# A shorter first softmax, and all taps of the first 32 columns summed on TensorE

## The chip, the cores and the metric

One core of one Trainium2 chip. The metric is the time of one execution on the device in microseconds (us), best read as a ratio to the kernel before, run in the same rounds on the same chip. Before: 417.61 us, median of 3 runs (417.58 to 418.06).

## The reference

Two stages, on 8 x 4160 tokens of 192 numbers. A dynamic convolution weighs, for each token and each of 8 heads, the token and its 6 predecessors with a softmax of 7 logits; then a maxout layer takes the larger of two products with 192 x 1024 weights and multiplies it by a third matrix.

```
w = exp(weight_gen - max);  w = w / sum(w)              # 8 heads x 7 taps
conv[b,s,h,:] = sum_k w[b,s,h,k] * x_pad[b,s+k,h,:]     # 24 channels a head
g = maximum(conv @ w1, conv @ w2)                       # 192 -> 1024
out = g @ w_out                                         # 1024 -> 192
```

## The kernel before

Each of the 128 partitions holds 260 consecutive tokens ("columns"), worked off in batches of 16. The work of a batch runs through the engines like this; the names are those of the profile:

```
exp_sum(b)     ScalarE  e_t = exp(wg_t)
red(b)         VectorE  sum_t = sums of 7
ln(b)          ScalarE  sum_t = ln(sum_t)
shift(b)       VectorE  wg_t -= sum_t          # from batch 3 on in 3 parts, between the additions
weights(b, o)  ScalarE  en_t = exp(wg_t)       # columns o..: the softmax weights, each twice
mul(b, o)      VectorE  m_t = x * en_t         # 7 taps x 8 columns x 192, 5.75 us
adds(b, o)     VectorE  the 7 taps added up into y_t
transpose(u)   DMA      yt = y_t transposed    # the "features" of TensorE
hidden(g, ..)  TensorE  hd = yt * (w2 - w1); ScalarE: rd_t = relu(hd)
               TensorE  op_ps = w1 w_out, yt + w_out, rd_t; ScalarE: o_t = op_ps, then the store
```

So two chains pass through ScalarE in turn: VectorE's (sum, logarithm, subtraction, exps, product) and TensorE's (features, relus, results). In the traces ScalarE runs its instructions in the order in which they are written: one that waits holds up what stands behind it (by 4.62 us in one case below).

The first 32 columns (batches 0 and 1) go in pieces of four, and TensorE itself transposes them and adds up taps, by multiplying m_t with the identity:

```python
LEFT = (0, 1, 2, K - 1)

def sum_transpose(u, taps=range(K)):
    ...
    for k in range(6):
        for t in taps:
            for r in range(2):
                ...
                nc.tensor.matmul(yps[:, ...], lhsT=m_t[half(r), at:at + P],
                                 rhs=ident[half(r), half(r)], ...)
    nc.scalar.copy(out=_sub(yt, ...), in_=_sub(yps, ...))

# later batches, hung on tile t of the hidden layer:
if s == 0 and b + 1 < NB:
    c = b + 1
    mul(c, 0)
    adds(c, 0, beside=lambda i, of: shift(c + 1, i, of) if c + 1 < NB else None)
if s == 8 and b + 2 < NB:
    mul(b + 1, 8)
    adds(b + 1, 8, beside=lambda i, of: red(b + 3, i, 2) if b + 3 < NB and i < 2 else None)
```

Five of the eight pieces go with LEFT: VectorE adds three taps onto three others (`adds(.., True)`), and TensorE sums four. The other three leave all seven to TensorE.

The softmax here doesn't subtract the row's maximum and nothing guards it: scores larger than these inputs give would overflow.

Of the kernel before, what the change touches and what calls it, by code (L numbers as in the profile page):

```python
# [9 lines left out]
FP32 = mybir.dt.float32  # L10
# [3 lines left out]
ALU = mybir.AluOpType  # L14
# [9 lines left out]
def kernel(  # L24
# [100 lines left out]
    def exp_sum(b):  # L125
        e_ts[b] = pe_.tile([P, BATCHES[b][1] * WGC], FP32, name="e_t", tag="e")
        nc.scalar.activation(out=e_ts[b], in_=wg_ts[b], func=AF.Exp)  # L127

    def part(b, i, of):

        n = BATCHES[b][1]
        h0, h1 = n * i // of * H, n * (i + 1) // of * H
        return slice(h0, h1), h0 * K, [[K, h1 - h0], [1, K]]

    def red(b, i=0, of=1):
        if i == 0:
            s_ts[b] = psm.tile([P, BATCHES[b][1] * H], FP32, name="sum_t", tag="sum")
        hs, at, ap = part(b, i, of)
        nc.vector.reduce_sum(out=s_ts[b][:, hs], in_=_sub(e_ts[b], at, ap), axis=AX.X)  # L139

    def ln(b):
        nc.scalar.activation(out=s_ts[b], in_=s_ts[b], func=AF.Ln)  # L142

    def shift(b, i=0, of=1):
        hs, at, ap = part(b, i, of)
        w_t = _sub(wg_ts[b], at, ap)
        nc.vector.tensor_tensor(out=w_t, in0=w_t, in1=_sub(s_ts[b], hs.start, [[1, hs.stop - hs.start], [0, K]]),  # L147
                                op=ALU.subtract)

    def weights(b, o):  # L150

        w = dict(pieces(b))[o]
        if b not in en_ts:
            en_ts[b] = pen.tile([P, 16 * WGC * 2], BF16, name="en_t", tag="en")
        J = 2 if w == 4 and b < 2 else 1
        N = w * H // J
        for j in range(J):
            nc.scalar.activation(  # L158
                out=_sub(en_ts[b], (o * WGC + j * N * K) * 2, [[2 * N, K], [2, N], [1, 2]]),
                in_=_sub(wg_ts[b], (o * H + j * N) * K, [[1, K], [K, N], [0, 2]]), func=AF.Exp,  # L160
            )


    def mul(b, o):

        n = dict(pieces(b))[o]
        if n == 4 and b < 2:
            m_out = _sub(m_t, K * o * D, [[64, 2], [P, K * 6], [1, 64]])
            x_in = _sub(xb_ts[b], o * D, [[2 * D, 2], [D, K], [1, 2 * D]])
        else:  # L170
            m_out = m_t[:, K * o * D:K * (o + n) * D]
            x_in = _sub(xb_ts[b], o * D, [[D, K], [1, n * D]])
        nc.vector.tensor_tensor(  # L173
            out=m_out, in0=x_in,
            in1=_sub(en_ts[b], o * WGC * 2, [[2, K * n * H], [0, G // 2], [1, 2]]),
            op=ALU.mult,
        )

    def adds(b, o, first=False, beside=lambda i, of: None):


        w = dict(pieces(b))[o]
        n = w * D

        def taps(at, step, cnt):
            return _sub(m_t, K * o * D + at * n, [[step * n, cnt], [1, w * D]])

        beside(0, 3)
        nc.vector.tensor_tensor(out=taps(0, 1, 3), in0=taps(0, 1, 3), in1=taps(3, 1, 3), op=ALU.add)  # L189
        if first:  # L190
            return
        beside(1, 3)
        if b not in y_ts:
            y_ts[b] = py.tile([P, 16 * D], BF16, name="y_t", tag="y")
        nc.vector.tensor_tensor(out=taps(0, 2, 2), in0=taps(0, 2, 2), in1=taps(1, 5, 2), op=ALU.add)  # L195
        beside(2, 3)

        nc.vector.tensor_tensor(  # L198
            out=_sub(y_ts[b], o * D, [[64, 2], [P, 3 * w // 2], [1, 64]]),
            in0=taps(0, 1, 1), in1=taps(2, 1, 1), op=ALU.add,  # L200
        )
# [24 lines left out]
    LEFT = (0, 1, 2, K - 1)  # L226

    def sum_transpose(u, taps=range(K)):

        b, o, n = UNITS[u]  # L230
        assert n == 4
        yps = ps["r" if "r" in ps else "o"].tile([P, 1024], FP32, name="yps", tag="op")
        for k in range(6):
            for t in taps:
                for r in range(2):
                    at = (K * o + t * n) * D + k * P
                    nc.tensor.matmul(  # L237
                        yps[:, r * 512 + k * 64:r * 512 + (k + 1) * 64],
                        lhsT=m_t[half(r), at:at + P], rhs=ident[half(r), half(r)],
                        start=(k == 0 and t == taps[0]), stop=(t == taps[-1]),  # L240
                        skip_group_check=True,
                    )
        yt = pyt.tile([P, 8 // 2 * 3 * P], BF16, name="yt", tag="yt")
        nc.scalar.copy(out=_sub(yt, 0, [[64, 2], [P, 6], [1, 64]]),  # L244
                       in_=_sub(yps, 0, [[512, 2], [64, 6], [1, 64]]))
        yt_ts[u] = yt

# [143 lines left out]
    OUTS, c = [[], [], []], 0  # L391
    for g in range(3, len(GROUPS)):
        most = 4 if g == 3 else 2 if GROUPS[g][1] == 2 or len(OUTS[-1]) == 4 else 4
        n = min(most, ready[g] - c)
        OUTS.append(list(range(c, c + n)))
        c += n
# [78 lines left out]
    with tc.tile_pool(name="pstage", bufs=1) as pstage:  # L475
# [5 lines left out]
        load_wg(0, nc.sync)  # L481
# [14 lines left out]
        load_first(0)  # L496
        HF = F // 2

        def load_w(h):
            for kind, r0, nr in (("E", 0, P), ("T", P, 64)):  # L500
                for wi, wsrc in enumerate((moe_w1, moe_w2)):
# [17 lines left out]
        exp_sum(0)  # L519
        red(0)  # L520
        ln(0)
        shift(0)
        xb_ts[0] = pxb.tile([P, (16 + PAD) * D], BF16, name="xb_t", tag="xb")
        nc.scalar.activation(out=xb_ts[0][:, 0:PAD * D], in_=xs[:, 0:PAD * D], func=AF.Copy,
                             scale=msk[:, 0:1])
        for o in (0, 4, 8, 12):
            weights(0, o)
        nc.vector.tensor_copy(out=xb_ts[0][:, PAD * D:(PAD + 4) * D],
                              in_=xs[:, PAD * D:(PAD + 4) * D])
        mul(0, 0)  # L530
        nc.scalar.copy(out=xb_ts[0][:, (PAD + 4) * D:(PAD + 8) * D], in_=xs[:, (PAD + 4) * D:])
# [3 lines left out]
        def w_diff(h, copy):  # L535

            c0, c1, c2 = (slice(s * F + h * HF, s * F + (h + 1) * HF) for s in range(3))
            nc.vector.tensor_tensor(out=wd[:, c0], in0=ws["E", 1][:, c0], in1=ws["E", 0][:, c0],
                                    op=ALU.subtract)
            copy(out=wd[64:P, c2], in_=wd[0:64, c0])  # L540
            copy(out=wd[0:64, c1], in_=wd[64:P, c0])
            nc.vector.tensor_tensor(out=wd[0:64, c2], in0=ws["T", 1][:, c0], in1=ws["T", 0][:, c0],
                                    op=ALU.subtract)
            copy(out=wd[64:P, c1], in_=wd[0:64, c2])


        nc.gpsimd.tensor_copy(out=gate[0:64, :], in_=ws["T", 1][:, 0:1])
        load_x(0, 8, 4)
        load_x(0, 12, 4)
# [3 lines left out]
        )  # L553
        load_x(1, 0, 8)
# [27 lines left out]
        keep_warm(115)  # L582
        w_diff(0, nc.scalar.copy)
        sum_transpose(0)
        keep_warm(14)
        mul(0, 4)


        nc.scalar.copy(out=w1["E"], in_=ws["E", 0])
        hidden(0)  # L590
        nc.scalar.copy(out=w1["T"], in_=ws["T", 0])
        w_diff(1, nc.vector.tensor_copy)
        mul(0, 8)
        adds(0, 8, True)
        sum_transpose(1)
        exp_sum(1)
        red(1)
        hidden(1)
        ln(1)
        shift(1)  # L600
        mul(0, 12)
# [20 lines left out]
        for h in range(2):  # L622
            nc.scalar.copy(out=w1t[:, 4 * h * D:4 * (h + 1) * D], in_=tp[:, h * 1024:h * 1024 + 4 * D])  # L623
        weights(1, 0)
        weights(1, 4)
        mul(1, 0)
        adds(1, 0, True)
        sum_transpose(2, LEFT)
        load_x(2, 0, 16)
        load_wg(4, nc.gpsimd)  # L630
        mul(1, 4)
        hidden(3)
        w10_product()
        exp_sum(2)
        red(2)
        adds(1, 4, True)
        sum_transpose(3)
        weights(1, 8)
        weights(1, 12)
# [5 lines left out]
    def rest_of_1():  # L645
        mul(1, 8)
        shift(2)
        adds(1, 8, True)
        mul(1, 12)

    def end_of_1():
        exp_sum(3)
        red(3)
        adds(1, 12, True)
# [4 lines left out]
        3: (none, rest_of_1),  # L659
        4: (lambda: sum_transpose(4, LEFT), lambda: (end_of_1(), weights(2, 0))),  # L660
        5: (lambda: sum_transpose(5, LEFT), none),
        6: (lambda: (weights(2, 8), ln(3), sum_transpose(6, LEFT)), lambda: load_x(3, 0, 8)),
        7: (lambda: sum_transpose(7, LEFT), none),
    }

    def extra(t):
# [9 lines left out]
        if s == 0 and b + 1 < NB:  # L676
# [3 lines left out]
            adds(c, 0, beside=lambda i, of: shift(c + 1, i, of) if c + 1 < NB else None)  # L680
        if s == 8 and b + 2 < NB:
            mul(b + 1, 8)
            adds(b + 1, 8, beside=lambda i, of: red(b + 3, i, 2) if b + 3 < NB and i < 2 else None)
# [11 lines left out]
    out_room(OUTS[3])  # L695
    go = relay(out_first(OUTS[3]))
    out_second(OUTS[3], go)
    ln(2)
    evac(OUTS[3][0] // 2, len(OUTS[3]) // 2)
    early[3][1]()  # L700
    for g in range(4, len(GROUPS)):
# [3 lines left out]
        if g in early:  # L705
# [36 lines left out]
```

## Time and profile before

| | before |
|---|---|
| median of 3 runs; the profiled run | 417.61 us; 418.47 us (span 416.7) |
| PE, DVE (VectorE), ACT (ScalarE) busy | 96%, 91%, 86% |
| VectorE's last result starts | 383.39 |
| the last hidden tiles (24 narrow matmuls) start | 398.42 |

The profiled run is 0.9 us slower than the median; it had a stage of half clock from 22.6 to 26.0 us, which not every run of this kernel has (see d1). From the page of the kernel before: the granted TensorE clock in 40 slices of the span, and the shares of the chain of work that ended last.

```profile
PEclk9989999999999999999999999999999999999999
...
PE 74%; ACT 18%; issue 4%; DMA 2%; SPq 1%; ACTq 1%; DVE 0%; DVEq 0%
```

By its second line VectorE has no part in what sets the end. From the waits of the kernel before (columns: us in total, times, longest) and VectorE's timeline (start, length; at the end of a line the idle time before it and what ended it):

```profile
DVE m_t L173 <- ACT en_t L158: 1.8, 2, 1.5
...
ACT en_t L158 <- DVE wg_t L147: 0.3, 1, 0.3
```

```profile
48.88 5.75 DVE L173 TENSOR_TENSOR m_t<-xb_t,en_t 128x10752 bf16<-128x10752 bf16 x1
...
59.83 0.95 DVE L198 TENSOR_TENSOR y_t<-m_t 128x1536 bf16<-128x1536 bf16 x1
60.70 5.75 DVE L173 TENSOR_TENSOR m_t<-xb_t,en_t 128x10752 bf16<-128x10752 bf16 x1
```

The first product of batch 2 starts at 48.88, and from there VectorE works without a pause, 11.82 us per 8 columns. The wait of 0.3 us, ScalarE's exps (en_t) waiting for VectorE's subtraction (wg_t), looks like nothing. It will turn out to be the line that mattered.

### The profile page before, as it was taken

Reading aid. Unit: us, or ns where it says so; the run is one execution under the profiler, and the core shown is the slowest. Engines: PE = TensorE matmul, PEld = TensorE weight load, DVE = VectorE, ACT = ScalarE, POOL = GpSimd, SP = SyncE. Lnnn points to the kernel's source line nnn. Section 1 sums busy time; section 2 is a strip of 40 time slices with the busy share of each in tenths; the row PEclk is TensorE's granted clock in tenths of the full one; section 3 lists DMA queues with packets and bytes.
Section 4 is the critical chain, followed back from the end, with each engine's and each line's share of the span. In section 5 each row is a group of like instructions: output and inputs, shape, how many; then the busy total and the mean of one; then the engine's idle time right before and its main releaser. Section 6 shows DMA issues by size and latency. Waiting matters only on the chain.

```text
span 416.7 us, 15924 instructions
## 1 busy us (share of the span) xinstructions
PE 398.3 (96%) x7369; PEld 323.7 (78%) x7369; DVE 377.2 (91%) x218; ACT 360.4 (86%) x424; POOL 74.4 (18%) x102
## 2 busy tenths in 40 slices
PE   7878899999999999999999999999999999999995
PEld 7767799777777778777777777777777787777795
DVE  5989999999999999999999999999999999998000
ACT  5888989999899899898989989899898988887871
POOL 1510102221201222122112222221013220210000
PEclk9989999999999999999999999999999999999999
DMA  8965418767588766874966678667776676474213
GB/s 250 264 155 165 91 63 187 138 167 163 134 162 175 185 164 155 196 164 139 219 138 157 170 136 237 140 169 192 124 219 111 148 193 151 116 164 118 95 51 142
DMA packets 60242, 65.68 MB, mean 158 GB/s; under 512 B 47601, under 2 KB 48497, under 8 KB 60176
## 3 DMA queue, kind: packets, MB, share of 16 engines
q0 software_dynamic: 8128, 24.11, 28.1%
q1 hardware_dynamic: 46720, 15.30, 20.8%
q10 hardware_dynamic: 5328, 25.27, 15.7%
q8 instruction: 57, 0.93, 0.9%
q14 instruction: 9, 0.07, 0.1%
HBM read 35.96 MB, written 25.56 MB: 148 GB/s over the span
## 4 chain that ended last, share of the span: by engine, by line
PE 74%; ACT 18%; issue 4%; DMA 2%; SPq 1%; ACTq 1%; DVE 0%; DVEq 0%
PE op_ps L312 34%; PE hd L272 31%; ACT rd_t L282 10%; PE op_ps L324 7%; ACT en_t L158 3%; PE hdp L272 2%; ACT o_t L368 2%; DMA ws1T<-in_moe_w_dram 2%; ACT e_t L127 1%; ACT yt L244 1%; ACTq L378 0%; PE yps L237 0%; SPq L502 0%; ACT w1t L623 0%; ACT w L617 0%
## 5 line engine op out<-in xcount | busy, mean ns | idle before, releaser
L282 ACT ACTIVATE rd_t<-hd 128x1024 bf16<-128x1024 f32 (+1 forms) x206 | 234.4, 1183 | 28.1 <-PE hd L272 27.6
L312 PE MATMUL op_ps<-wo,rd_t 64*128 64x192 bf16 x4160 | 210.6, 243 | 0.1
L312 PEld LDWEIGHTS <-rd_t 64*128 64x128 bf16 x4160 | 180.4, 94 | 15.9 <-ACTq L345 0.3
L173 DVE TENSOR_TENSOR m_t<-xb_t,en_t 128x10752 bf16<-128x10752 bf16 (+1 forms) x37 | 187.7, 5072 | 1.8 <-ACT en_t L158 1.8
L272 PE MATMUL hd<-yt,wd 64*128 64x512 bf16 (+1 forms) x1584 | 187.4, 360 | 0.9 <-ACT rd_t L282 0.9
L272 PEld LDWEIGHTS <-wd 64*128 64x128 bf16 x1776 | 95.3, 95 | 42.1 <-issue 2.7
L213 POOL CAST gate<-yt 128x1 f32<-128x1 bf16 x29 | 38.7, 1335 | 274.6 <-DMA yt<-y_t 274.6
L189 DVE TENSOR_TENSOR m_t<-m_t 128x4608 bf16<-128x4608 bf16 (+1 forms) x34 | 79.6, 2341 | 0.1
L368 ACT COPY o_t<-op_ps 128x384 f32<-128x384 f32 (+1 forms) x99 | 57.2, 588 | 8.2 <-PE op_ps L312 8.1
L324 PE MATMUL op_ps<-w,yt 64*128 64x192 bf16 x780 | 55.5, 243 | 5.7 <-ACT o_t L368 2.2
L324 PEld LDWEIGHTS <-yt 64*128 64x128 bf16 x780 | 38.7, 94 | 23.0 <-issue 8.7
L195 DVE TENSOR_TENSOR m_t<-m_t 128x3072 bf16<-128x3072 bf16 (+1 forms) x29 | 50.0, 1725 | 0.1
L158 ACT ACTIVATE en_t<-wg_t 128x896 bf16<-128x896 f32 (+2 forms) x45 | 34.8, 803 | 2.2 <-ACT o_t L368 1.7
L198 DVE TENSOR_TENSOR y_t<-m_t 128x1536 bf16<-128x1536 bf16 (+1 forms) x29 | 27.3, 942 | 0.5
L358 DVE COPY o_t<-op_ps 128x192 f32<-128x192 f32 x1 | 0.4, 358 | 28.7 <-ACT o_t L358 28.7
L147 DVE TENSOR_TENSOR wg_t<-wg_t,sum_t 128x280 f32<-128x280 f32 (+4 forms) x45 | 22.0, 490 | 0.8 <-ACT sum_t L142 0.8
L139 DVE TENSOR_REDUCE sum_t<-e_t 128x64 f32<-128x448 f32 (+2 forms) x30 | 19.6, 654 | 2.5 <-ACT e_t L127 2.5
L115 POOL DMA_DIRECT2D xb_t<-in_x_dram x32 | 17.2, 538 | 25.2 <-DVE m_t L173 17.2
L282 ACT ACTIVATE rd_t<-hdp 128x1024 bf16<-128x1024 f32 x16 | 15.9, 1029 | 3.6 <-PE hdp L272 2.8
L127 ACT ACTIVATE e_t<-wg_t 128x896 f32<-128x896 f32 (+1 forms) x17 | 15.8, 930 | 2.9 <-DMA wg_t<-in_weight_gen_dram 2.4
L272 PE MATMUL hdp<-yt,wd 64*128 64x256 bf16 x192 | 14.2, 288 | 1.1 <-issue 0.7
L579 PE MATMUL warm<-ident 128*128 128x128 bf16 x129 | 10.4, 260 | 3.0 <-DVE ident L518 3.0
(45 smaller groups left out, 81.6 us busy)
## 6 DMA issues: line engine op xcount, KB each, us to landing
out_dram<-o_t ACTq DMA_DIRECT2D x28, 768.0 KB, 3.9
xb_t<-in_x_dram POOLq DMA_DIRECT2D x28, 384.0 KB, 5.0
wg_t<-in_weight_gen_dram POOLq DMA_DIRECT2D x14, 448.0 KB, 6.2
xb_t<-xb_t POOLq DMA_DIRECT2D x16, 288.0 KB, 5.7
out_dram<-o_t ACTq DMA_DIRECT2D x8, 384.0 KB, 2.8
wg_t<-in_weight_gen_dram SPq DMA_DIRECT2D x2, 448.0 KB, 5.3
xs<-in_x_dram SPq DMA_DIRECT2D x2, 384.0 KB, 6.3
xb_t<-in_x_dram POOLq DMA_DIRECT2D x1, 768.0 KB, 7.0
```

Of the source, the lines that this page charges most:

```text
L147: nc.vector.tensor_tensor(out=w_t, in0=w_t, in1=_sub(s_ts[b], hs.start, [[1, hs.stop - hs.start], [0, K]]), op=ALU.subtract)
L158: nc.scalar.activation(out=_sub(en_ts[b], (o * WGC + j * N * K) * 2, [[2 * N, K], [2, N], [1, 2]]), in_=_sub(wg_ts[b], (o * H + j * N) * K ...
L173: nc.vector.tensor_tensor(out=m_out, in0=x_in, in1=_sub(en_ts[b], o * WGC * 2, [[2, K * n * H], [0, G // 2], [1, 2]]), op=ALU.mult,)
L189: nc.vector.tensor_tensor(out=taps(0, 1, 3), in0=taps(0, 1, 3), in1=taps(3, 1, 3), op=ALU.add)
L195: nc.vector.tensor_tensor(out=taps(0, 2, 2), in0=taps(0, 2, 2), in1=taps(1, 5, 2), op=ALU.add)
L198: nc.vector.tensor_tensor(out=_sub(y_ts[b], o * D, [[64, 2], [P, 3 * w // 2], [1, 64]]), in0=taps(0, 1, 1), in1=taps(2, 1, 1), op=ALU.add,)
L213: nc.gpsimd.tensor_copy(out=gate, in_=yt[:, 0:1])
L272: nc.tensor.matmul(hid_out(t, f, j), lhsT=wd[half(j), s * F + f * P:s * F + (f + 1) * P], rhs=_sub(yt_ts[u][half(j), :], (s + j) % 3 * P, ...
L282: nc.scalar.activation(out=rd[:, k * 1024:(k + n) * 1024], in_=hd[:, at:at + n * 1024], func=AF.Relu)
L312: return nc.tensor.matmul(op_out(c), lhsT=rd[half(r), k * 1024 + at:k * 1024 + at + P], rhs=wo[half(r), f * D:(f + 1) * D], start=False, s ...
L324: nc.tensor.matmul(op_out(c + j), lhsT=yt_ts[u][half(j), (3 * i + (s + j) % 3) * P:(3 * i + (s + j) % 3 + 1) * P], rhs=w10[half(j), s * D: ...
L368: nc.scalar.copy(out=_sub(o, c % 24 * D, [[D, len(qs)], [h * D, 2], [1, D]]), in_=_sub(tile_, at + (qs[0] - p) * D, [[D, len(qs)], [512, 2 ...
```

## The change

The intent is a shorter start. The softmax of the first four columns is worked out alone, from a logits load of 112 KB instead of 448, so that TensorE gets features earlier. All seven taps of the first 32 columns are summed on TensorE, which takes five additions off VectorE. Copies, casts and loads of the prologue are reordered, and the first results are computed a group later.

```diff
-    LEFT = (0, 1, 2, K - 1)
-    def sum_transpose(u, taps=range(K)):
+    def tap_sums(u, k0=0, k1=K):          # always all taps; unit 0 in two parts
+    def features(u):                      # the copy to yt apart from it
...
-    OUTS, c = [[], [], []], 0
-    for g in range(3, len(GROUPS)):
+    OUTS, c = [[], [], [], []], 0
+    for g in range(4, len(GROUPS)):
...
-        load_wg(0, nc.sync)
+        load_logits(0, 4)
         load_first(0)
+        load_logits(4, 12)
...
-        exp_sum(0); red(0); ln(0); shift(0)
-        for o in (0, 4, 8, 12): weights(0, o)
-        mul(0, 0)
+        exp_sum(0, 0, 4); red(0, first); ln(0, first); shift(0, first); weights(0, 0)
+        exp_sum(0, 4, 12)
+        mul(0, 0, (0, 4)); red(0, rest); ln(0, rest); mul(0, 0, (4, K))
...
-        keep_warm(115); w_diff(0, ..); sum_transpose(0); keep_warm(14); mul(0, 4)
-        hidden(0); ...
+        keep_warm(75); tap_sums(0, 0, 4); keep_warm(8); tap_sums(0, 4, K)
+        cast_w1(0); shift(0, rest); features(0); weights(0, 4); w_diff(0, ..)
+        hidden(0); mul(0, 4); keep_warm(20); tap_sums(1); ...
...
     early = {
-        3: (none, rest_of_1),                                        # mul(1,8) shift(2) mul(1,12)
-        4: (.. sum_transpose(4, LEFT), .. (end_of_1(), weights(2, 0))),  # exp_sum(3) red(3)
-        6: (.. (weights(2, 8), ln(3), sum_transpose(6, LEFT)), .. load_x(3, 0, 8)),
-        7: (.. sum_transpose(7, LEFT), none),
+        5: (.. (exp_sum(2), red(2), mul(1, 8), sum_transpose(4)), .. weights(1, 12)),
+        6: (.. (ln(2), shift(2), mul(1, 12), sum_transpose(5)), .. (exp_sum(3), red(3), load_x(3, 0, 8))),
+        7: (.. sum_transpose(6), .. (weights(2, 0), sum_transpose(7))),
+        8: (.. (weights(2, 8), ln(3)), none),
     }
```

(Cut to its core, several statements on a line, ".." for "lambda:".) Note the last part: the exps and the logarithm that feed VectorE for batches 2 and 3 come two to three groups later than before.

## The prediction

> **What bounds the kernel now.** I read the page first, then busy time by stretches, the waits of TensorE, the timeline of the first 60 us, and the timeline of the end.
>
> ```profile
> PE 398.3 (96%) x7369; PEld 323.7 (78%) x7369; DVE 377.2 (91%) x218; ACT 360.4 (86%) x424; POOL 74.4 (18%) x102
> ```
>
> Three engines look nearly full, so shares alone decide nothing. Busy time by stretch (us; then busy and count of PE, PEld, DVE, ACT, POOL; clock; DMA share; GB/s):
>
> ```profile
> 24.00:25.00 1.00, 1.00 (x14) 0.94 (x10) 1.00 (x2) 0.10 (x1) 0.00 (x0) 0.50 1.03 302
> ...
> 30.00:40.00 10.00, 7.79 (x251) 7.19 (x251) 9.97 (x6) 8.48 (x18) 0.00 (x0) 1.00 0.64 172
> ...
> 100.00:150.00 50.00, 49.28 (x858) 38.35 (x856) 49.93 (x29) 44.94 (x51) 10.62 (x15) 1.00 0.73 173
> ```
>
> From about 57 us on, TensorE hardly pauses. VectorE doesn't either, but it is ahead:
>
> ```profile
> 383.39 0.56 DVE L198 TENSOR_TENSOR y_t<-m_t 128x768 bf16<-128x768 bf16 x1
> ...
> 398.42 1.49 PE L272 MATMUL hd<-yt,wd 64*128 64x256 bf16 x24
> ```
>
> VectorE's last result is ready at 384.0; with 4.2 us of DMA transpose (its median) it could be used at 388, and TensorE gets to it at 398.4. So VectorE has some 10 us to spare at the end, TensorE sets the pace, and a microsecond gained before 57 us counts only if TensorE gets it. What is lost there: the timeline gives 41 ns per 192-wide matmul (32 in 1.32 us), 108 ns at 512 wide (12 in 1.30), 55 ns at 256 wide (24 in 1.31), 14.6 ns per tap matmul (84 in 1.23). The counts between 12.3 and 77.5 us come to 430+84 at 41, 384 at 55, 492 at 14.6, 6 at 108 and about 3.7 us of warming, transposes and the w1 product: 53.8 of 65.2 us. So 11.4 us are lost there, against about 1.4% from 77.5 us on. The waits name part of them:
>
> ```profile
> PE tp L567 <- issue: 2.3, 1, 2.3
> PE op_ps L324 <- ACT o_t L368: 2.2, 5, 0.5
> PE op_ps L324 <- ACT w L617: 1.8, 1, 1.8
> PE op_ps L324 <- ACT yt L244: 1.7, 2, 0.9
> ```
>
> The stall of 2.3 us is the transpose of w1 waiting for ScalarE's cast; behind it the clock is 0.50 for about 3.3 us. The others wait for ScalarE too. **In the start ScalarE is the bound, not VectorE**: from its first features (14.23) to the end of the copy of group 8's results (58.6) it idles about 5.8 of 44.4 us.
>
> ```profile
> 14.23 0.80 ACT L244 CAST yt<-yps 128x768 bf16<-128x768 f32 x1
> ...
> 19.55 0.79 ACT L244 CAST yt<-yps 128x768 bf16<-128x768 f32 x1
> ...
> 54.32 0.50 ACT L368 COPY o_t<-op_ps 128x384 f32<-128x384 f32 x1
> ...
> 58.12 0.50 ACT L368 COPY o_t<-op_ps 128x384 f32<-128x384 f32 x1
> ...
> 58.70 0.43 PE L324 MATMUL op_ps<-w,yt 64*128 64x192 bf16 x6
> ```
>
> The last row is my measuring point: TensorE starts group 9's results as soon as ScalarE has copied group 8's. From there on both kernels do the same work.
>
> [...]
>
> **The change, part by part.**
>
> (a) First softmax. The logits of four columns are 112 KB instead of 448, so I take 2.5 us to landing (the 96 KB store takes 2.5): 3.2 instead of 4.4. Exp 0.4, sum 0.3, ln 0.2, subtract 0.3, four exps 1.0: done at 5.5. Then the x load binds: it landed at about 7.4 and has 336 KB less ahead of it, 1.0 us at 330 GB/s, so 6.4. Copy to 7.25; four taps of the product, 4/7 of 2.95, to 9.0; tap matmuls to 9.7 (75 warming matmuls end at 9.0). The remaining sums (0.8) and three taps (1.3) end at 10.95, their matmuls at 11.55. First features at 11.8 instead of 14.2: **2.4 us earlier**.
>
> (b) What was ahead of the features is now behind them: six of the exps of batch 0 (1.9 us) and two copies of the weight difference (1.24), while half of the w1 casts (1.05) go ahead. ScalarE's load behind its first features rises by 2.1 us. That takes back nearly all of (a).
>
> (c) Hidden group 0 needs ScalarE's weight copy (13.8) and runs to 14.4. In the built order its second tile waits on ScalarE where it waited on TensorE: the warming tile is used again afterwards and keeps its buffer, so the tile follows the first relu (15.7) and ends at 16.4. Then 20 warming matmuls, 1.6 us, to 18.0. The second product begins later, for VectorE has first the rest of the subtraction (0.85), the weight difference (1.9) and a copy (0.5): 14.0 to 16.9, against 12.8 to 15.7. Its tap matmuls end at 19.2, the features start at 19.4, against 19.55. **At this point the lead is 0.15 us.**
>
> (d) From 19.4, in ScalarE's order at the trace's spacing: features 0.7, casts 1.05, relus 1.8, exp 0.85, exps 0.6, relus 1.8, w1 copy 1.4, ln 0.3, features 0.7, relus 1.8 (to 30.3), w1 product 1.4, exps 1.2, relus 1.8, features 0.7: 35.4. The first results' second half waits for that point, 1.3 us; their copy ends at 37.7 (before: 38.5, with group 4 not yet done). Groups 5 to 7 cost ScalarE 4.2 to 4.8 us each (relus 1.8, features 0.7, copy 0.45, one or two exps, a DMA issue): group 7's copy ends at 51.0 instead of 54.8, with two columns fewer done. The 2.3 us stall and its slow clock should be gone, for the casts are done in halves ahead of need.
>
> (e) Group 8 gives it back: an exp (0.95), the eighth tap sum and features (to 53.2), the relus of two tiles (53.8 to 55.6), four columns instead of two (0.8 us more on TensorE in each half), the last relu (57.3), an exp and an ln now ahead of the copy (1.2), a copy of 0.85: about 59.2 instead of 58.6. The count of columns is equal again here.
>
> (f) TensorE gets 5 units x 36 = 180 tap matmuls, 180 x 14.6 ns = 2.6 us, all before 57 us and mostly where it waits for ScalarE. VectorE loses five additions at 1.28 us spacing, 6.4 us, but then waits for ScalarE: I get 52 us for its first product of batch 2, against 48.9. That eats 3 of its 10 us and does not bind.
>
> Sum: 417.6 + (59.2 - 58.6) = 418.2 with nothing gained from the vanished slow clock beyond the steps above. I round several waits upward, and the order inside a group hides some of them, so I allow 1.7 us the other way: **416.5 us**.
>
> **Rivals.** *The start is worth what it looks like.* If ScalarE idles less than I think in groups 4 to 8, the 2.4 us of (a) and the 1.7 us lost at half clock both reach the end: 413 to 414. For it: 11.4 us are lost in the start. Against it: (b), work moved and not removed. *A new slow spell.* In my times TensorE has little between 11.6 and 15.7; if the clock halves there, warming and tap matmuls stretch and the features of unit 1 come 1 to 2 us later: 419 to 420. [...] *VectorE binds.* It waits for ScalarE's exps in batch 1, and a start of batch 2 after 58 us would use up its reserve; then each microsecond later is one at the end: 420 or more. *TensorE's added taps count in full*: 2.6 us more, 420; against it, TensorE waits in just these groups.
>
> **Range and chances.** The first rival sets the lower end, the second and fourth the upper: 413.2 to 419.6. A gain of 2% is 8.4 us, over 70% of all that is lost in the start, and (b) makes it unlikely: 0.03. A loss of 2% would need VectorE to bind: 0.02. Within 2%: 0.95.
>
> **What would show it.** Right: first features near 11.8, second near 19.4; no stall ahead of w1's transposes; ScalarE busy over 90% from 20 to 36 us; group 7's copy near 51, group 9's results near 59; the same pace from there; TensorE's end about as far behind VectorE's as now, less 3 us. Wrong: a lead at group 9 over 4 us or a delay over 2; a clock of 0.50 after 12 us; a TensorE that waits on transposed features late in the run.

## The result, and the profile after

The changed kernel is correct and slower: 427.96 us, median of 4 runs (426.58 to 428.65), all in the fast state. The ratio is 1.0245, 95% interval 1.0215 to 1.0275. Ratios here are the mean time of one kernel's fast runs over that of the other's fast runs of the same rounds, so not quite the ratio of the medians quoted. The predicted 416.5 us was missed by 11.5 us, the upper end of its range (413.2 to 419.6) by 8.4.

From the page of the kernel after: busy time, clock, and the chain that ended last.

```profile
PE 403.3 (95%) x7523; PEld 325.3 (76%) x7523; DVE 372.7 (87%) x218; ACT 359.4 (84%) x427; POOL 78.5 (18%) x102
...
PEclk9699989999999999999999999999999999999998
...
DVE 66%; PE 20%; ACT 8%; issue 4%; DMA 1%; SPq 0%; ACTq 0%; DVEq 0%
```

VectorE does 4.5 us less work than before, and yet two thirds of the chain that sets the end are now VectorE's, where it had none. The same end as in the prediction's view, after:

```profile
392.46 0.56 DVE L209 TENSOR_TENSOR y_t<-m_t 128x768 bf16<-128x768 bf16 x1
```
```profile
407.50 1.49 PE L292 MATMUL hd<-yt,wd 64*128 64x256 bf16 x24
```

VectorE is 9.07 us later (383.39), TensorE 9.08 (398.42). The distance is 15.04 us, before 15.03. Both came late together.

**Where VectorE's 9.07 us come from.** Every result of VectorE from batch 2 on is 9.07 to 9.08 us later than in the kernel before, the first as much as the last, so all of it was lost before 64 us. VectorE's timeline after:

```profile
26.50 1.09 DVE L142 TENSOR_REDUCE sum_t<-e_t 128x128 f32<-128x896 f32 x1 [3.46 <-ACT e_t L130]
...
35.00 5.83 DVE L186 TENSOR_TENSOR m_t<-xb_t,en_t 128x5376 bf16<-128x5376 bf16 x2 [3.42 <-ACT en_t L170]
43.30 1.09 DVE L142 TENSOR_REDUCE sum_t<-e_t 128x128 f32<-128x896 f32 x1 [2.47 <-ACT e_t L130]
...
53.39 5.76 DVE L186 TENSOR_TENSOR m_t<-xb_t,en_t 128x10752 bf16<-128x10752 bf16 x1 [1.28 <-ACT en_t L170]
63.62 0.45 DVE L152 TENSOR_TENSOR wg_t<-wg_t,sum_t 128x280 f32<-128x280 f32 x1 [4.47 <-ACT sum_t L147]
```

Four times VectorE waits over a microsecond for an exp on ScalarE, so that it starts batch 2 at 53.39 instead of 48.88: 4.5 us. Then it waits 4.47 us for the logarithm of batch 3 (sum_t). Together 9.0.

**Why the logarithm is late.** The timeline of all engines after, around 60 us (rows left out):

```profile
55.84 0.41 PE L332 MATMUL op_ps<-wo,rd_t 64*128 64x192 bf16 x6
...
59.09 0.98 PE L332 MATMUL op_ps<-wo,rd_t 64*128 64x192 bf16 x10 [2.84 <-issue]
...
61.45 1.02 ACT L302 ACTIVATE rd_t<-hd 128x1024 bf16<-128x1024 f32 x1 [4.62 <-PE hd L292]
62.38 1.01 ACT L170 ACTIVATE en_t<-wg_t 128x896 bf16<-128x896 f32 x1
...
63.28 0.31 ACT L147 ACTIVATE sum_t<-sum_t 128x128 f32<-128x128 f32 x1
```

TensorE stops for 2.84 us in the middle of a run of equal matmuls, with nothing named that it waits for ("issue"). ScalarE's next relu therefore comes at 61.45, and the logarithm stands behind it: ScalarE idles 4.62 us with the logarithm's input long ready (its sums were done at 52.1).

**What the stall is.** The queue that the profile calls "instruction" (q8) moved 59 packets of 16 KB in the kernel after, and one of them falls into this stall. The transfers of the kernel after from 52.35 us to this packet, in 40 slices, and then behind it:

```profile
DMA  0099496570390598289979795999889899696830
...
q0 software_dynamic: 220, 0.68, 88.8%
```
```profile
q8 instruction: 1, 0.02, 5.5%
q0 software_dynamic: 4, 0.00, 1.2%
```

For 4.4 us almost nothing but the x load of batch 3 (two issues at 51.41 and 51.94) moved. The instruction packet came at 56.74, right behind the last of it, ended at 57.72, and TensorE went on at 59.08, 1.36 us after its end. In the stall of 2.28 us of the kernel before the times are alike: a packet from 20.32 to 21.30, and TensorE went on at 22.67, 1.37 us after its end. That TensorE waited for this packet, and the packet for the load, is a reading of these times; a2 tests it.

**The start.** Busy time by stretch (us; then busy and count of PE, PEld, DVE, ACT, POOL; clock; DMA share; GB/s), before and then after:

```profile
10.00:15.00 5.00, 4.64 (x142) 4.40 (x140) 5.00 (x4) 3.93 (x8) 3.77 (x5) 1.00 1.06 314
15.00:20.00 5.00, 4.25 (x134) 3.84 (x134) 4.86 (x7) 4.18 (x6) 1.80 (x4) 1.00 1.31 202
```
```profile
10.00:15.00 5.00, 2.78 (x80) 2.15 (x73) 4.76 (x8) 3.31 (x7) 3.46 (x5) 0.94 1.06 308
15.00:20.00 5.00, 3.89 (x36) 2.92 (x35) 4.62 (x5) 3.19 (x5) 0.00 (x0) 0.50 1.29 195
```

TensorE has little to do from 10 to 15 us, its granted clock is 0.50 from 14.4 to 21.3 (6.83 us), and from 15 to 20 it gets through 36 matmuls where it did 134. The second features start at 21.97 instead of 19.55.

### The profile page after: what moved, and what is told of

Read it like the earlier page. It is cut to its first block, busy times and chain, and to the rows that moved or that the text cites. A ratio compares the mean times of both kernels' runs of the same rounds, so it can differ in the third digit from the quotient of the medians.

```text
span 426.5 us, 16240 instructions
## 1 busy us (share of the span) xinstructions
PE 403.3 (95%) x7523; PEld 325.3 (76%) x7523; DVE 372.7 (87%) x218; ACT 359.4 (84%) x427; POOL 78.5 (18%) x102
## 4 chain that ended last, share of the span: by engine, by line
DVE 66%; PE 20%; ACT 8%; issue 4%; DMA 1%; SPq 0%; ACTq 0%; DVEq 0%
DVE m_t L186 33%; DVE m_t L202 14%; DVE m_t L206 10%; PE op_ps L332 9%; PE hd L292 7%; ACT rd_t L302 3%; DVE sum_t L142 3%; DVE wg_t L152 3%; DVE y_t L209 3%; PE op_ps L344 2%; ACT en_t L170 1%; DMA xs<-in_x_dram 1%; ACT yt L259 1%; PE yps L249 1%; PE hdp L292 1%
## 5 line engine op out<-in xcount | busy, mean ns | idle before, releaser
L186 DVE TENSOR_TENSOR m_t<-xb_t,en_t 128x10752 bf16<-128x10752 bf16 (+3 forms) x38 | 187.7, 4943 | 6.0 <-ACT en_t L170 5.1
L224 POOL CAST gate<-yt 128x1 f32<-128x1 bf16 x29 | 42.8, 1477 | 273.9 <-DMA yt<-y_t 273.9
L202 DVE TENSOR_TENSOR m_t<-m_t 128x4608 bf16<-128x4608 bf16 (+1 forms) x29 | 72.8, 2511 | 0.1
L170 ACT ACTIVATE en_t<-wg_t 128x896 bf16<-128x896 f32 (+4 forms) x47 | 35.4, 776 | 3.6 <-ACT o_t L388 1.7
L152 DVE TENSOR_TENSOR wg_t<-wg_t,sum_t 128x280 f32<-128x280 f32 (+6 forms) x46 | 22.2, 483 | 4.8 <-ACT sum_t L147 4.8
L142 DVE TENSOR_REDUCE sum_t<-e_t 128x64 f32<-128x448 f32 (+4 forms) x31 | 19.8, 638 | 6.4 <-ACT e_t L130 6.4
L130 ACT ACTIVATE e_t<-wg_t 128x896 f32<-128x896 f32 (+2 forms) x18 | 16.0, 887 | 2.9 <-DMA wg_t<-in_weight_gen_dram 1.9
L249 PE MATMUL yps<-ident,m_t 64*128 64x64 bf16 x672 | 12.0, 193 | 0.8 <-ACT yt L259 0.4
```

The source lines that it names most:

```text
L152: nc.vector.tensor_tensor(out=w_t, in0=w_t, in1=_sub(s_ts[b], hs.start, [[1, hs.stop - hs.start], [0, K]]), op=ALU.subtract)
L170: nc.scalar.activation(out=_sub(en_ts[b], (o * WGC + (J * k0 + j * (k1 - k0)) * N) * 2, [[2 * N, k1 - k0], [2, N], [1, 2]]), in_=_sub(wg_t ...
L186: nc.vector.tensor_tensor(out=m_out, in0=x_in, in1=_sub(en_ts[b], (o * WGC + k0 * n * H) * 2, [[2, (k1 - k0) * n * H], [0, G // 2], [1, 2] ...
L202: nc.vector.tensor_tensor(out=taps(0, 1, 3), in0=taps(0, 1, 3), in1=taps(3, 1, 3), op=ALU.add)
L224: nc.gpsimd.tensor_copy(out=gate, in_=yt[:, 0:1])
```

## The experiments

The theory after the first look ("VectorE theory"): the end follows the moment at which VectorE starts batch 2 and gets the logarithm of batch 3, because VectorE has no reserve. The rivals: the stall of TensorE at 56 us and the clock ("stall theory", "TensorE theory"), or the added taps. All runs, with the two ends named above (VectorE's last result, the last hidden tiles) where the profile is of the fast state:

| run | median us | ratio to before | VectorE's last | TensorE | apart |
|---|---|---|---|---|---|
| before | 417.6 | 1 | 383.39 | 398.42 | 15.03 |
| after | 427.96 | 1.0245 | 392.46 | 407.50 | 15.04 |
| a1, logarithm early | 424.48 | 1.0166 | 388.30 | 403.66 | 15.36 |
| a2, load later | 425.45 | 1.0225 | 388.40 | 403.44 | 15.04 |
| a3, both | 424.52 | 1.0174 | 387.96 | 403.00 | 15.04 |
| e1, a3 + VectorE's order | 423.68 | 1.0132 | 385.22 | 400.38 | 15.16 |
| f1, a3 less a product | 422.09 | 1.0107 | 385.91 | 401.43 | 15.52 |
| b2, before + 2.9 us VectorE | 419.88 | 1.0052 | 384.82 | 399.87 | 15.05 |
| f2, before less a late product | 417.59 | 0.9995 | 378.87 | 398.02 | 19.15 |
| d1, before, loads later | 417.17 | 1.0002 | 382.28 | 397.33 | 15.05 |
| d2, before, all taps | 419.99 | 1.0066 | 383.35 | 399.01 | 15.66 |
| d3, d2 + d1 | 420.53 | 1.0068 | 381.51 | 396.90 | 15.39 |
| b1, before + 5.7 us VectorE | 424.13 | 1.0146 | slow | slow | - |
| c1, a3 + warming moved | 427.35 | 1.0161 | slow | slow | - |

The last column is the key to the case: 15.04 us apart is where TensorE runs on VectorE's heels, for in b2, a2, a3 and after, whose chain of work is VectorE's, it is 15.04 to 15.05 throughout. The kernel before stands at 15.03, which suggests that its reserve was not 10 us but none; b1 and b2 test it.

### a1: the logarithm of batch 3 ahead of the stall

```diff
-        7: (.., lambda: (weights(2, 0), sum_transpose(7))),
-        8: (lambda: (weights(2, 8), ln(3)), none),
+        7: (.., lambda: (weights(2, 0), ln(3), sum_transpose(7))),
+        8: (lambda: weights(2, 8), none),
```

> The changed kernel with the logarithm of batch 3's sums moved from group 8 to the end of group 7, nothing else. VectorE theory (its late batch 2 sets the end, by 9.08 us: 4.5 from the late first product, 4.5 from the wait for this logarithm): the wait goes, VectorE's lag behind the kernel before falls to about 4.6, TensorE keeps its stall of 2.8 us in group 8 and its lag of 5.5 us, and the time falls by about 3.5 us to some 424.4. Stall theory (the stall in group 8 and the half clock behind it are the loss, VectorE has reserve): the time stays within 0.5 us of the changed kernel's 428.

Measured: 424.48 (423.92 to 425.24), ratio 1.0166 [1.0144, 1.0187]; as the VectorE theory had it. The stall of TensorE stays (2.23 us of idle matmul, 2.84 in the kernel after), and still 3.3 us come back. VectorE's wait after, in the waits of this run:

```profile
DVE wg_t L152 <- ACT sum_t L147: 0.3, 1, 0.3
```

### a2 and a3: the load that the instruction packet stood behind, later

```diff
-            lambda: (exp_sum(3), red(3), load_x(3, 0, 8))),
+            lambda: (exp_sum(3), red(3))),
...
+    def gated_load():                     # called in group 8
+        nc.gpsimd.tensor_copy(out=gate, in_=rd_at[16][0][:, 0:1])
+        load_x(3, 0, 8)
```

> The changed kernel with the load of x for batch 3 held back until group 8's first relu. If the 2.84 us stall of TensorE in group 8 is an instruction fetch that queues behind this load, the stall is gone, no half clock follows it, and TensorE's lag at group 9 is about 1 us instead of 5.6. The logarithm of batch 3 then also comes in time. VectorE theory: VectorE is still about 4.5 us late from its first product of batch 2, which sets the end: about 422.5. Stall theory: about 418.5. If the stall has another cause, it stays and the time is 428.

Measured: 425.45 (424.85 to 430.15), ratio 1.0225 [1.0162, 1.0288]. The stall is gone; TensorE's timeline of this run, at the place where it stopped:

```profile
54.89 0.84 PE L332 MATMUL op_ps<-wo,rd_t 64*128 64x192 bf16 x16
55.55 0.43 PE L344 MATMUL op_ps<-w,yt 64*128 64x192 bf16 x6
55.80 0.84 PE L332 MATMUL op_ps<-wo,rd_t 64*128 64x192 bf16 x16
56.46 0.83 PE L292 MATMUL hd<-yt,wd 64*128 64x256 bf16 x12
```

With the load moved, the packet comes at 53.2 us, where it came at 56.74 in the kernel after, and TensorE doesn't stop: this is what the stall was. Yet the time is not the 418.5 us of the stall theory: that falls. The 422 to 422.5 us of the VectorE theory are missed too, by 3 us here and by 2 in a3; in the profiled run (424.87, 6.4 us above the profile of before) VectorE's lag is 5.0 us, and the other 1.4 lie behind the last hidden tiles. TensorE is only 1.3 us behind the kernel before at 140 us, but 2.0 at 237, 3.5 at 283, 4.3 at 330 and 5.0 at 376, where it has met VectorE, which was 5.01 behind from the start.

> Both edits. VectorE theory: as with the gated load alone, 422 to 422.5, for without the stall the logarithm was not waited for. Stall theory: 418.5.

Measured with both mends: 424.52 (423.16 to 427.31), ratio 1.0174 [1.0131, 1.0217], no better than a1 alone. VectorE's results are 4.58 us late throughout, and TensorE's lag grows from 1.15 us to the same 4.58.

### b1 and b2: the kernel before, with more work for VectorE alone

```diff
             mul(c, 0)
+            if c == 2:
+                mul(c, 0)
```

> The kernel before with VectorE's first product of batch 2 computed twice (same result), 5.7 us more for VectorE and nothing else. VectorE theory (no reserve at the end: ScalarE's exps of batch 15 wait for VectorE already): 5 to 5.7 us slower, 423. The prediction's reserve of 10 us: no change, within 0.5 us of 417.6.

Measured: 424.13 (one run of four, the profiled one, in the slow state, 429.21; the fast ones 422.87 to 425.26), ratio 1.0146 [1.0111, 1.0182], 6.1 us. A reserve of 10 us would have hidden it. As that profile was slow, the dose was halved:

```diff
     def rest_of_1():
         ...
         mul(1, 12)
+        mul(1, 12)
```

> The kernel before with the last product of batch 1 computed twice on VectorE (2.9 us more there, same result, nothing else changed). VectorE theory (no reserve at the end): 2.0 to 2.9 us slower than before, 419.5 to 420.3. If VectorE had the 10 us of reserve that the prediction gave it: same time, within 0.3 us.

Measured: 419.88 (419.79 to 419.91), ratio 1.0052 [1.0033, 1.0071]: 2.2 us of 2.9. In its profile VectorE starts batch 2 at 50.34, 1.46 us later than before, and that run (419.91) is 1.44 us above the profiled run of before. The dose cost its 2.9 us in full: ahead of it, at 42.22, VectorE was 1.5 us earlier than in the profile of before (43.76): this run had no half clock near 22 us, and the wait of 1.5 us for en_t that before has at 29.22 was not there. TensorE runs 0.0 us behind the kernel before up to tile 192, at 306 us, and 1.44 us behind at tile 224, 354 us. What happens between, in the timelines of the kernel before, of b2 and of after, near 345 us:

```profile
341.38 0.44 DVE L147 TENSOR_TENSOR wg_t<-wg_t,sum_t 128x280 f32<-128x280 f32 x1
341.86 1.04 ACT L158 ACTIVATE en_t<-wg_t 128x896 bf16<-128x896 f32 x1 [0.34 <-DVE wg_t L147]
342.80 1.00 ACT L282 ACTIVATE rd_t<-hd 128x1024 bf16<-128x1024 f32 x1
```
```profile
342.83 0.44 DVE L147 TENSOR_TENSOR wg_t<-wg_t,sum_t 128x280 f32<-128x280 f32 x1
...
343.30 1.04 ACT L158 ACTIVATE en_t<-wg_t 128x896 bf16<-128x896 f32 x1 [1.08 <-DVE wg_t L147]
...
344.25 1.00 ACT L282 ACTIVATE rd_t<-hd 128x1024 bf16<-128x1024 f32 x1
```
```profile
350.46 0.44 DVE L152 TENSOR_TENSOR wg_t<-wg_t,sum_t 128x280 f32<-128x280 f32 x1
350.93 1.03 ACT L170 ACTIVATE en_t<-wg_t 128x896 bf16<-128x896 f32 x1 [0.80 <-DVE wg_t L152]
```

This is the link. ScalarE's exps of batch 15 need the second part of VectorE's subtraction, which VectorE does between the additions of batch 14. ScalarE waits for it, and the relu that TensorE needs stands behind. Looked up in the trace of the kernel before, the time from the end of that second part to the exps is 7.3 us at batch 3, 4.3 at 6, 2.9 at 9, 1.5 at 12 and 0 at 15 (every third batch; those between have 1 to 2.4 us more, and shrink alike). It must shrink: VectorE takes 23.67 us per 16 columns (its results, 60.8 to 344.8), TensorE 23.03 (its hidden tiles, 76.06 to 398.41). So the kernel before meets VectorE just at its end, and any delay of VectorE moves the meeting forward and lengthens the run. The same wait comes in two more forms in b2: 1.05 us at 308.12, where the logarithm waits for VectorE's sums, and 0.41 at 322.66, where exps wait for a y_t.

In the kernel after, VectorE holds TensorE in a second way too, from 155 us on, where it was not yet late enough for this one. From its timeline (the first line is GpSimd's small cast, which reads the transposed features to know that they are there):

```profile
162.26 7.97 POOL L224 CAST gate<-yt 128x1 f32<-128x1 bf16 x1 [11.70 <-DMA yt<-y_t]
162.27 1.47 PE L292 MATMUL hd<-yt,wd 64*128 64x512 bf16 x12 [1.18 <-ACT o_t L388]
```

VectorE's result was ready at 152.71, its transposition landed only just before 162.26, 9.5 us later (4.2 is the median before), and TensorE's hidden tile starts in the same moment; the releaser named, ScalarE's copy, ended 0.1 us earlier. TensorE's lag goes from 5.50 to 6.86 us here, to 7.89 near 230 (0.69 us behind ScalarE, whose exps had waited 0.91 us for a logits load, and 0.31 us for features again), and in two more steps, with ScalarE's waits for VectorE about them (0.79, 0.41 and 0.80 us), to 8.62 and 9.08.

### e1: VectorE's order of work before batch 2

On top of a3, products no longer stand behind a sum that waits for ScalarE, and the exps of batch 2 go ahead of a group's end:

```diff
-        5: (lambda: (exp_sum(2), red(2), mul(1, 8), sum_transpose(4)), ..),
-        6: (lambda: (ln(2), shift(2), mul(1, 12), sum_transpose(5)), lambda: (exp_sum(3), red(3))),
-        7: (.., lambda: (weights(2, 0), ln(3), sum_transpose(7))),
+        5: (lambda: (exp_sum(2), mul(1, 8), red(2), sum_transpose(4)), ..),
+        6: (lambda: (ln(2), mul(1, 12), shift(2), sum_transpose(5)), lambda: (exp_sum(3), red(3), weights(2, 0))),
+        7: (.., lambda: (ln(3), sum_transpose(7))),
```

> Both mends (ln of batch 3 early, the load behind the prologue's stretch) and, on top of them, VectorE's work for batches 1 and 2 put in another order, so that its products do not stand behind a sum that waits for ScalarE's exps: the first product of batch 2 should start near 50.7 us instead of 53.46. Nothing is taken from TensorE or added to it. VectorE theory (the end follows VectorE's start of batch 2): VectorE's results 1.8 us behind those of the kernel before instead of 4.58, and the time about 2.7 us under the 424.5 us of both mends, so 421 to 422.5. TensorE theory (the end follows TensorE's lag at group 9, 1.1 us): unchanged, 424 to 425.

Measured: 423.68 (421.38 to 424.07), ratio 1.0132 [1.0099, 1.0165]. VectorE did what was meant, from this run's timeline:

```profile
50.68 5.75 DVE L186 TENSOR_TENSOR m_t<-xb_t,en_t 128x10752 bf16<-128x10752 bf16 x1
```

Its results are 1.8 us behind the kernel before, as expected, and in the chain of work PE has 66% again. The profiled run (421.38) has the time that the VectorE theory asked for; the other three (423.5 to 424.1) don't, so the median missed by over a microsecond. From 1.0174 to 1.0132 the direction is right, but the intervals overlap.

### f1 and f2: a product left out

The results of these two are wrong on purpose (relative errors 0.2 and 0.33); all other engines keep their work. f1 is a3 without the second product of batch 2; f2 is the kernel before without that of batch 12:

```diff
-            mul(b + 1, 8)
+            if b + 1 != 2:                # f2: != 12
+                mul(b + 1, 8)
```

> Both mends, and the second product of batch 2 on VectorE left out (5.7 us of VectorE's time; the result is wrong on purpose, TensorE, ScalarE and the transfers keep all their work). VectorE theory: VectorE's results come about 1.1 us before those of the kernel before instead of 4.58 us behind, TensorE's lag stays at its 1.1 to 1.2 us to the end, and the time is 418 to 419.5 us. If TensorE's own work or its clock made the end late: 424 to 425 as with both mends.

Measured: 422.09 (421.56 to 422.87), ratio 1.0107 [1.0085, 1.0129]. That is below both mends (1.0174), so VectorE did hold those back, by 2.8 us. But it is 3 us above what was expected, and 15.52 apart says that VectorE hardly binds any more, though its chain of work still has DVE 43%: VectorE itself ends 2.5 us behind the kernel before instead of 1.1 ahead, having waited 1.75 us for a logarithm at 104 us, and at 332 us a transposition of 8.8 us adds 0.35 us to TensorE's lag. TensorE's lag is already 2.9 us at 79 us and stays near that, 3.0 at the end. One cause of it, in this run's timeline:

```profile
37.05 0.42 PE L332 MATMUL op_ps<-wo,rd_t 64*128 64x192 bf16 x6 [2.27 <-issue]
```

An instruction packet came here too (34.68; TensorE went on 2.37 us after it came, in the kernel after 2.34), at a place where the profiles of a3 and of after have no such stall. So TensorE's own start and end cost some 4.5 us here, where the theory had 1.1.

> The kernel before with the second product of batch 12 on VectorE left out (5.7 us of VectorE's time near 280 us; wrong result on purpose). In the kernel before VectorE's lead over ScalarE's exps is used up only near batch 15 (about 340 us), so if VectorE and TensorE are just balanced there, there is little to win: 0 to 0.6 us faster, 416.7 to 417.3. If VectorE already holds the kernel before back, several us faster (414 or less).

Measured: 417.59 (416.77 to 418.6), ratio 0.9995 [0.9965, 1.0026]. With 5.7 us less for VectorE to do TensorE gains nothing: in the kernel before the two engines are balanced, neither is ahead by anything worth having.

### d1, d2, d3: parts of the change in the kernel before

d1 moves three loads of the prologue behind the second hidden group, for the stall of 2.3 us at 20 us, which the prediction put down to a cast:

```diff
-        load_wg(2, nc.gpsimd); load_x(1, 8, 8); load_wg(3, nc.gpsimd)
...
         hidden(1)
+        nc.gpsimd.tensor_copy(out=gate, in_=rd_at[2][0][:, 0:1])
+        load_wg(2, nc.gpsimd); load_x(1, 8, 8); load_wg(3, nc.gpsimd)
```

> The kernel before with three loads (logits 2 and 3, half of x of batch 1) held back from 18.7 us to group 1's first relu, about 22. If the 2.3 us stall of TensorE at 20.4 is an instruction fetch behind loads, it shrinks below 1 us and no half clock follows (22.6 to 26.0). VectorE theory: VectorE has no reserve and TensorE's gain counts only as far as ScalarE brings VectorE's batch 2 forward, about 1.5 us: 415.5 to 417. Stall theory (TensorE sets the end): up to 4 us faster, 413.

Measured: 417.17 (416.97 to 418.66), ratio 1.0002 [0.998, 1.0025]. A miss: the stall did not shrink below 1 us.

```profile
22.18 0.27 PE L564 MATMUL tp<-ident,w1E 128*128 128x128 bf16 x2 [1.77 <-issue]
```

The packet came at 19.79 instead of 20.32, and the slow clock behind the stall went away in this run (granted clock 0.998). But with these loads in place the stall is 1.69 us in b2 and 1.73 in d2, without a slow clock either, and with them moved it is 2.15 in d3, with one: the move changed nothing that can be told from this scatter. It looks like 1.1 us against the profile of before, but that profile is of a run at 418.47. The runs of the kernel before fall in two kinds by their granted clock: 14 at 0.996 or more took 416.8 to 417.8 us, 7 at 0.995 or less took 417.9 to 418.5, and the profiled one (0.994) is of the second. That the stall is not the cast is shown by the cast having ended at 15.97. That it is a wait for a packet was the author's reading, from TensorE going on 2.35 us after the packet came in the kernel before and 2.39 in d1, as in the kernel after (2.34); that these loads cause it is not shown.

d2 has TensorE sum all taps in the kernel before (LEFT holds all seven, the five additions are dropped), and d3 adds d1's move:

```diff
-    LEFT = (0, 1, 2, K - 1)
+    LEFT = tuple(range(K))
```

> The kernel before with only one part of the change: all taps of the first 32 columns on TensorE (five additions fewer on VectorE, 6.4 us; 180 tap matmuls more on TensorE, 2.6 us). VectorE's batch 2 starts 2 to 6 us earlier, as far as ScalarE's exps allow. TensorE then sets the end: within 1 us of before if the taps fill waits, 2.6 us slower if they count in full. So between 416 and 420; a new stall would show as an idle gap with an instruction packet in it.

Measured: 419.99 (419.06 to 421.6), ratio 1.0066 [1.0034, 1.0098]: 2.8 us slower, against 2.6 us of added tap matmuls. That the taps count in full does not follow from it: in the profiled run (419.06) TensorE's last hidden tiles are only 0.59 us behind the kernel before, and it stops for 1.68 us more at 27.8 us ("issue"). VectorE gets no lasting lead from the additions saved; its waits in this run have grown instead:

```profile
DVE sum_t L139 <- ACT e_t L127: 5.2, 3, 2.5
DVE wg_t L147 <- ACT sum_t L142: 4.1, 5, 1.9
```

Its first result of batch 2 is 4.7 us earlier than before, its third 2.3, and from the ninth on it is level: what it may do is set by when ScalarE makes exps and logarithms.

> The kernel before with all taps on TensorE and the loads held back. VectorE theory: now VectorE has the reserve that lets TensorE's gain count: faster than either alone, 413 to 415. If TensorE's added taps count in full: 416.

Measured: 420.53 (416.94 to 422.9), ratio 1.0068 [1.0011, 1.0124]: the same as d2, with a wide spread; the profiled run (416.94) is as fast as the fastest of the kernel before. Both expectations were missed: a lead of VectorE did not let TensorE's gain count.

### c1: more warming matmuls

On top of a3, 24 warming matmuls ahead of the first hidden group instead of 20 behind it.

```diff
         tap_sums(0, 4, K)
+        keep_warm(24)
...
-        keep_warm(20)
```

> Both edits of the earlier run, and the 20 warming matmuls behind hidden group 0 go to the gap ahead of it (24 there), which also frees the buffer that made the group's second tile wait for a relu. If the half clock from 14.4 to 21.3 us [...] delays the second features (22.0 in the changed kernel, 19.4 in the prediction), it is gone and they come near 19.4; ScalarE is then 2 to 2.5 us earlier, VectorE's first product of batch 2 starts near 51 instead of 53.4. VectorE theory: the end follows by the same 2 to 2.5 us, to about 422 against 424.5 for both edits. If the slow clock is hidden behind ScalarE's work anyway: no change.

Measured: 427.35, with two of four runs (428.59, the profiled one, and 430.81) in the slow state and the fast ones 426.1 and 422.14; ratio 1.0161 [1.0102, 1.022]. Inconclusive: nothing is read from it, and that warming matmuls in that gap keep the clock up is not shown.

No version tried beats the kernel before.

## Why the prediction was wrong

**The step that failed** is the reserve: "So VectorE has some 10 us to spare at the end", and in (f) "That eats 3 of its 10 us and does not bind". The 10 us were read from the last transposed features alone. VectorE also feeds ScalarE, and the exps of a batch need VectorE's subtraction a batch ahead of the features; that link had 0 us left at batch 15 (the wait of 0.34 us). b2 (2.2 us slower for 2.9 us of work on VectorE) and b1 (6.1 for 5.7) show it, and f2 that there was no debt either. Nor was the 4.2 us of transposition, a median, safe to count on: one took 9.5. What the prediction had named as a sign against itself, "a TensorE that waits on transposed features late in the run", is there in the kernel after at 162 and 232 us. So the third rival came true, with its limit wrong: not "a start of batch 2 after 58 us" but anything after 48.9. The chance given to a loss of 2% was 0.02, with the right condition beside it ("would need VectorE to bind"). The other signs of being wrong came too: a delay over 2 at group 9 (its results start at 64.38 instead of 58.70), half clock after 12 us (from 14.4).

**VectorE's start of batch 2** was put at 52 and came at 53.39. The size was nearly right; with the right reserve the sum would have said some 3 us slower. **The logarithm**: (e) has "an exp and an ln now ahead of the copy (1.2)" as ScalarE's load only. That VectorE waits for that very logarithm, 4.47 us, was not seen; a1 gives 3.3 us back for moving it.

**The stall.** "The stall of 2.3 us is the transpose of w1 waiting for ScalarE's cast" was a misreading of "issue", which names no releaser: the cast had ended at 15.97, TensorE stopped at 20.39, and it went on 1.37 us after the end of an instruction packet (21.30). So "the 2.3 us stall and its slow clock should be gone, for the casts are done in halves" had no ground. That stall did not appear in the kernel after, but one of 2.84 us came at 56 us. In the kernel after the instruction packets are as little as 3.4 us apart up to there (38.36 and 41.76), and 7.3 on average from 104.8 us on; whether the added tap matmuls made this stall was not tested.

**What was right.** (a): first features predicted at 11.8, measured at 12.02 (VectorE's parts there add up to 11.1, not 10.95, which changes little). (b): "That takes back nearly all". (c) was 2.6 us off (19.4, measured 21.97), by the trace for the most part because the second rival's slow spell came, 14.4 to 21.3: the 20 warming matmuls took 2.32 us instead of 1.6, the tap matmuls 1.97 instead of 1.4. (d): group 7's copy at 51.0, measured 51.94 to 52.44. (e): group 8 starts at 53.37, 0.49 us ahead of before; its end would have been near 59.2, and is, in a3 where the stall is gone, 60.15, 1.5 us behind the kernel before rather than 0.6. **(f), TensorE's half**: whether the 2.6 us of taps fell "mostly where it waits" stays open: in d2, alone in the kernel before, they came with a loss of 2.8 us, but its profile shows TensorE only 0.59 us late. The fourth rival is neither shown nor ruled out.

**The account of 10.2 us** (ratio 1.0245): 3.0 for the logarithm behind the stall (after against a3), 2.8 for VectorE's late start (a3 against f1), 4.5 for TensorE's own start and end (f1 against before); the intervals of a3 and f1 make these good to some 2 us. Of the last, 0.7 to 1.4 us lie in the last store, which took 3.1 to 3.9 us from issue to landing in those profiles of the changed kernel and its variants that were looked up, and 2.4 to 2.5 in those of the kernel before and its variants; why was not tested. The rest may be the added taps, stalls like the one at 37 us in f1 (2.27 us) and the slow clock; how it divides stays open, for the stalls move from run to run.

## What to carry to other kernels

A reserve is to be measured at every link by which an engine feeds others, at the latest batch and not just at the last output: between two engines of nearly equal pace a wait of 0.3 us on a third one can be the point where they meet, and giving one engine a few microseconds more is the quick test. A change that speeds up a start should leave alone, or move earlier, whatever feeds the engine that has no reserve; here exps and a logarithm that went two to three groups later cost more than the additions saved. "Issue" in front of an engine that runs through many short instructions is to be checked against the instruction packets and against what the other queues move at that time: here a packet came at 56.74 us behind 0.68 MB of loads, and at 53.2 with the load moved.
